# A kernel that plans its own instruction order: when a tile counts as free is taken from all its operations, not from the one scheduled last

## The chip, the cores and the metric

The kernel runs on one core of one Trainium2 chip. The metric is device time in microseconds (us) of one execution; lower is better. Three runs of the kernel before and one profiled execution of it are at hand.

## The reference

Attention with capped scores, followed by two dense stages, all in float32. `q`, `k`, `v` have shape 4 x 12 x 448 x 64 (48 heads).

```
s = cap * tanh(q @ k.T / 8 / cap);  p = exp(s - max);  a = p / sum(p) @ v
x = heads of a side by side                 # 1792 tokens x 768
h = x @ w_in;  x = (h * cos(h)) @ w_out     # 768 -> 2048 -> 768
x = ((x @ w1) * (x @ w2)) @ w3 @ w_out2     # 768 -> 1024 -> 1024 -> 768
```

The weights come as 64-bit floats and are turned into float32 on the chip.

## The kernel before

**Numbers.** Most products are made at more than one multiplication's precision: each operand is split into a high part (a cast to the reduced-width float32 that TensorE takes) and a low part (what the cast left), and three matmuls (high by high, high by low, low by high: `mm3`, lines 389 to 391) are summed. So each weight and each activation needs a copy and a subtraction before TensorE can use it. The scores of the first four pairs of heads are made from plain float32 operands instead (`SLIM = 4`, line 604); both kernels do this.

**Stages.** Scores, tanh and exp of a pair of heads (lines 640 to 665), products with `v` (684, 689), division by the row sums, split (`a_out`); beside it `make_w34` multiplies `w3` and `w_out2` into one matrix. From about 180 us `moe1` runs beside what is left of attention: per unit TensorE makes `h` (`bank<-xh,wih`), the chain of `cos` runs on ACT, DVE and POOL (`hs`, `w`, `kk`, `g`), and TensorE multiplies by `w_out` (`bank<-g,woh`). The last stage, `moe2`, begins near 730 us.

**A weight's way** (`f64`, line 925, and `convert`, line 896). SP loads the 64-bit words (`raw` or `rawc`); ACT or POOL scales the high word (903, 904); POOL or DVE begins the float32 value in tile `x` or `wx` (line 909); DVE adds bits twice (916, 920). Then three operations read that tile: a transfer to DRAM (`spill`, issued by SP on line 385, so that a later pass need not convert again: `wi_d`, `wo_d`), the copy to the high part (`copy`, lines 365, 366 and 369), and the subtraction for the low part (`lo`, line 375). There are two tiles `x` and two tiles `wx`. In `rights` (line 1200) the same is done with four tiles `stl` and the transfer `w_d`.

**The order of the work.** The program first makes a list of operations with due times, costs and the engines on which each may run. `Plan.schedule` then plays them through in time with these costs: at each step it takes the operations in order of due time, and starts those whose inputs are ready, whose engine is idle and for which each new tile has a free slot in its ring. The sequence it finds is the order of the instructions; on the chip each engine runs its own in that order, and waits where a tile isn't free yet. A transfer is costed as 0.66 us on SP, then `kb / 250` on a common line, then 2.2 us:

```
out = end
if o.kb:
    line = max(line, end) + o.kb / self.RATE
    out = line + self.LATENCY
```

and `HOP` is 0.25 us. A tile goes back to its ring when the last of its operations has been scheduled.

Of the kernel before, what the change touches and what calls it, by code (L numbers as in the profile page):

```python
# [45 lines left out]
class Ref:  # L46
    def __init__(self, item, sub=None, pick=None):
        self.item, self.sub, self.pick = item, sub, pick
# [12 lines left out]

class Item:
    def __init__(self, ring):
        self.ring, self.slot, self.ops, self.first = ring, None, 0, None
        self.writers, self.readers = {}, {}

    def tile(self):
# [70 lines left out]
class Plan:  # L138
# [57 lines left out]
    def schedule(self):  # L196
        for o, after, before in self.events:
            for p in after:
                o.deps.update(p.users)
            for p in before:  # L200
                for u in set(p.users):
                    u.deps.add(o)
        for n, o in enumerate(self.ops):
            o.left = len(o.deps)
            for d in o.deps:
                d.nexts.append(o)
        free = dict(PE=1.0, ACT=2.0, DVE=3.4, POOL=1.5, SP=1.2, port=0.0)

        def port(x):
            return x[0] == "POOL" or len(x) > 3  # L210

        free[None] = 0.0
        table, order, t, line = "exp", [], 0.0, 0.0
        cands = [(o.due, n, o) for n, o in enumerate(self.ops) if o.left == 0]
        num = {o: n for n, o in enumerate(self.ops)}
        soon = []
        cands.sort(key=lambda c: c[:2])
        done, end_all = 0, 0.0
        busy = {e: 0.0 for e in free}
        while done < len(self.ops):  # L220
            while soon and soon[0][0] <= t + 1e-9:
                _, n, o = heapq.heappop(soon)
                cands.append((o.due, n, o))
            cands.sort(key=lambda c: c[:2])
            idle = {e for e in free if free[e] <= t + 1e-9}
            wait, rest, again, short = {}, [], False, set()
            for c in cands:
                o = c[2]
                if o.table and table and o.table != table and o.due > t - SLACK_T and any(
                        x[2].table == table for x in cands):  # L230
                    rest.append(c)
                    continue
                pick = min(o.opts, key=lambda x: max(free[x[0]] - t, free["port"] - t if port(x) else 0.0, 0.0) + wait.get(x[0], 0.0) + x[1] * (PAR.get("w" + (x[0] or ""), 1.0) if o.due < PAR["tw"] else 1.0))
                if pick[0] in idle and port(pick) and free["port"] > t + 1e-9:
                    pick = None
                elif pick[0] not in idle:
                    if len(o.opts) == 1:
                        wait[pick[0]] = wait.get(pick[0], 0.0) + pick[1] * PAR["back"]
                    pick = None
                need = {}  # L240
                for it in o.allocs:
                    need[it.ring] = need.get(it.ring, 0) + 1
                lack = {r for r, n in need.items() if sum(x[0] <= t + 1e-9 for x in r.free) < n}
                if pick is None or any(it.slot is None and it.first is not o for it in o.uses if it.ring) or any(
                        not r.loose and r.queue[0].first is not o for r in need) or lack or short & need.keys():
                    short |= {r for r in lack if r.loose}
                    rest.append(c)
                    continue
                for it in o.allocs:
                    it.ring.queue.remove(it)  # L250
                    it.slot = heapq.heappop(it.ring.free)[1]
                (e, cost, f), two = pick[:3], port(pick)
                if o.table:
                    if table != o.table:
                        cost += self.SWITCH
                    table = o.table
                end = t + cost
                if e is not None:
                    free[e] = end
                    idle.discard(e)  # L260
                    busy[e] += cost
                    if two:
                        free["port"] = end
                        busy["port"] += cost
# [4 lines that stand above are left out]
                end_all = max(end_all, out)  # L269
                if o.move is not None:  # L270
                    for k in o.move[1](o.allocs[0].slot):
                        heapq.heappush(o.move[0].free, (out, k))
                for it in o.uses:
                    it.ops -= 1
                    if it.ops == 0 and it.ring is not None:
                        heapq.heappush(it.ring.free, (out + (self.HOP if e else 0.0), it.slot))
                for x in o.nexts:
                    x.left -= 1
                    x.ready = max(x.ready, out + (self.HOP if e else 0.0))
                    if x.left == 0:  # L280
                        heapq.heappush(soon, (x.ready, num[x], x))
                order.append((t, f))
                done += 1
                again = again or e is None
            cands = rest
            if again:
                continue
            times = [x for x in free.values() if x > t + 1e-9]
            if soon:
                times.append(soon[0][0])  # L290
            times += [r.free[0][0] for r in self.rings if r.free and r.free[0][0] > t + 1e-9]
            if done < len(self.ops):
                assert times, [(c[0], [(it.ring.tag, it.ring.queue[0] is it, it.ring.free) for it in c[2].allocs])
                               for c in cands[:20]]
                t = max(t, min(times))
        self.time, self.busy = end_all, busy
        return order
# [1098 lines left out]
```

## Time and profile before

| what | value |
|---|---|
| three runs, median (lowest, highest) | 1071.6 us (1068.7, 1073.46) |
| the profiled execution, time | 1074.96 us |
| its span in the profile | 1073.2 us |
| TensorE busy (PE) | 1052.1 us, 98% |
| VectorE busy (DVE) | 860.9 us, 80% |
| ScalarE busy (ACT) | 492.9 us, 46% |
| GpSimd busy (POOL) | 177.5 us, 17% |
| granted TensorE clock, mean | 0.994 |

Times in the trace count from the start of the span. PEld is TensorE's weight load, SPq the queue of SyncE, which issues the transfers. "a <- b" names the tile written and the tiles read, with buffer numbers left out. PEclk is the granted TensorE clock as a share of its full 2.4 GHz.

### The profile page before, as it was taken

What the parts mean: (1) busy time and instruction counts of PE and PEld (TensorE: products, weight loads), DVE (VectorE), ACT (ScalarE), POOL (GpSimd) and SP (SyncE); (2) the same over time, 40 slices, a digit from 0 to 9 for tenths busy, and PEclk for the clock granted to TensorE, in tenths of its full rate; (3) what the DMA queues carried; (4) which work ended last, traced back from release to release, by engine and by line L of the source; (5) the groups of instructions that cost most, each with busy time, mean ns of one, the idle gap of its engine ahead of it and who ended that gap; (6) DMA issues with size and microseconds to landing.
All of it is one profiled execution on the core that took longest, in us unless ns stands there. A gap on an engine that the chain in (4) does not pass through costs nothing.

```text
span 1073.2 us, 15589 instructions
## 1 busy us (share of the span) xinstructions
PE 1052.1 (98%) x5808; PEld 892.4 (83%) x5808; DVE 860.9 (80%) x1317; ACT 492.9 (46%) x653; POOL 177.5 (17%) x165
## 2 busy tenths in 40 slices
PE   7999999999999999999999999999999999999997
PEld 2676775777777888889999999999999999999996
DVE  5888667897998999778789987779899889767642
ACT  6687666776676775632253211112443245311121
POOL 4221211321341222210001100011313100000000
PEclk9999998999999999999999999999999999999999
DMA  8866965866766764527633411205555446221132
GB/s 253 215 211 177 247 179 162 224 179 206 220 201 205 230 172 148 174 61 250 211 119 104 148 49 55 60 15 175 198 193 195 155 124 220 102 89 59 60 108 86
DMA packets 82120, 167.38 MB, mean 156 GB/s; under 512 B 19571, under 2 KB 55411, under 8 KB 82035
## 3 DMA queue, kind: packets, MB, share of 16 engines
q1 hardware_dynamic: 82034, 166.30, 50.7%
q8 instruction: 47, 0.77, 0.3%
q14 instruction: 39, 0.31, 0.1%
HBM read 127.47 MB, written 38.62 MB: 155 GB/s over the span
## 4 chain that ended last, share of the span: by engine, by line
PE 83%; DVE 7%; DMA 4%; issue 2%; ACT 1%; POOL 1%; SPq 1%; DVEq 0%; POOLq 0%; ACTq 0%
PE bank L389 24%; PE bank L391 24%; PE bank L390 24%; PE bank L684 5%; PE double L650 2%; PE double L651 2%; PE bank L689 2%; DMA raw<-in_w3T 1%; DMA wo_d<-wx 1%; DMA raw<-in_w_out 1%; SPq L385 1%; DMA rb<-rs_d 1%; DVE wx L916 1%; DVE ks L375 1%; DVE ql L375 1%
## 5 line engine op out<-in xcount | busy, mean ns | idle before, releaser
L389 PE MATMUL bank<-g,woh 128*128 128x448 f32 x384 | 140.2, 365 | 2.0 <-ACT zs L365 2.0
L389 PE MATMUL bank<-xh,wih 128*128 128x448 f32 x384 | 140.1, 365 | 0.9 <-DVE y L366 0.9
L391 PE MATMUL bank<-xh,wil 128*128 128x448 f32 x384 | 139.6, 364 | 0.0
L391 PE MATMUL bank<-g,wol 128*128 128x448 f32 x384 | 139.4, 363 | 0.0
L390 PE MATMUL bank<-xl,wih 128*128 128x448 f32 x384 | 139.0, 362 | 0.0
L390 PE MATMUL bank<-g,woh 128*128 128x448 f32 x384 | 138.7, 361 | 0.0
L375 DVE TENSOR_TENSOR y<-bank,y 128x448 f32<-128x448 f32 x168 | 103.4, 617 | 42.4 <-PE bank L391 41.3
L365 ACT COPY hs<-bank 128x448 f32<-128x448 f32 x73 | 39.0, 536 | 180.7 <-PE bank L391 180.5
L665 ACT ACTIVATE double<-double,ts 112x896 f32<-112x896 f32 x96 | 93.7, 982 | 61.6 <-PE double L651 52.7
L665 ACT ACTIVATE p<-double,pac 112x896 f32<-112x896 f32 x96 | 96.2, 1013 | 1.6
L389 PEld LDWEIGHTS bank<-g,woh 128*128 128x128 f32 x384 | 72.0, 188 | 12.6 <-ACT zs L365 2.4
L684 PE MATMUL bank<-p,v 112*32 112x448 f32 x768 | 80.9, 562 | 0.0
L389 PEld LDWEIGHTS bank<-xh,wih 128*128 128x128 f32 x384 | 72.3, 188 | 8.7 <-issue 2.2
L391 PEld LDWEIGHTS bank<-xh,wil 128*128 128x128 f32 x384 | 72.4, 188 | 5.2
L390 PEld LDWEIGHTS bank<-xl,wih 128*128 128x128 f32 x384 | 72.2, 188 | 5.1
L391 PEld LDWEIGHTS bank<-g,wol 128*128 128x128 f32 x384 | 72.1, 188 | 5.2
L390 PEld LDWEIGHTS bank<-g,woh 128*128 128x128 f32 x384 | 71.9, 187 | 4.9
L389 PE MATMUL bank<-ab,w34h 128*128 128x448 f32 x192 | 69.7, 363 | 0.0
L391 PE MATMUL bank<-ab,w34l 128*128 128x448 f32 x192 | 69.5, 362 | 0.0
L390 PE MATMUL bank<-ab,w34h 128*128 128x448 f32 x192 | 69.3, 361 | 0.0
L684 PEld LDWEIGHTS bank<-p,v 112*32 112x32 f32 x768 | 22.9, 113 | 47.0 <-issue 45.1
L650 PE MATMUL double<-qh,ks 128*112 128x448 f32 x160 | 59.5, 372 | 2.4 <-ACT p L665 2.2
(230 smaller groups left out, 2351.1 us busy)
## 6 DMA issues: line engine op xcount, KB each, us to landing
rawc<-in_w_out SPq DMA_DIRECT2D x16, 768.0 KB, 5.8
stq<-w_d SPq DMA_DIRECT2D x32, 384.0 KB, 3.2
rawc<-in_w_in SPq DMA_DIRECT2D x13, 768.0 KB, 5.2
qr<-in_q SPq DMA_DIRECT2D x41, 224.0 KB, 4.6
kr<-in_k SPq DMA_DIRECT2D x41, 224.0 KB, 4.3
raw<-in_w3T SPq DMA_DIRECT2D x16, 512.0 KB, 5.7
rawl<-in_w SPq DMA_DIRECT2D x10, 768.0 KB, 4.8
raw<-in_w_out SPq DMA_DIRECT2D x8, 768.0 KB, 6.6
```

What stands on the lines that cost most here:

```text
L365: "A": ("ACT", (0.051 if psum else 0.094) + n / 1200, lambda: ACT.copy(dst(), src())),
L375: "D": ("DVE", 0.068 + n / 960, lambda: DVE.tensor_tensor(dst(), a(), b(), op=op))
L385: plan.op(due, [("SP", 0.66, lambda: SP.dma_start(dst(), src()))], r=r, w=w, kb=kb)
L389: PE.matmul(out, wh, xh, start=first, stop=False, skip_group_check=on)
L390: PE.matmul(out, wh, xl, start=False, stop=False, skip_group_check=on)
L391: PE.matmul(out, wl, xh, start=False, stop=last, skip_group_check=on)
L650: PE.matmul(o, w, qh(), start=True, stop=False)
L651: PE.matmul(o, w, ql(), start=False, stop=True)
L665: lambda f=f, x=x, o=o: ACT.activation(o(), s(), f, scale=x[:CP]))],
L684: PE.matmul(pv()[q * Q:(q + 1) * Q, :S], w()[:, j, c, d:d + Q], piece(j, c), **flags)
L689: PE.matmul(z()[q:q + Q, :S], one(), piece(j, 2 * c + k), start=c == 0, stop=c == NT - 1)
L916: DVE.scalar_tensor_tensor(xi, h_(), 3, xi, op0=ALU.logical_shift_left, op1=ALU.bitwise_or)
```

## The change

Each tile keeps the latest end of the operations scheduled on it so far (`it.free`), and that time, not the end of the operation scheduled last, is when its slot goes back to the ring. The two differ where an operation scheduled earlier ends later. Nothing is added to or taken from the list of operations, their costs, due times or rings.

```
 class Item:
     def __init__(self, ring):
-        self.ring, self.slot, self.ops, self.first = ring, None, 0, None
+        self.ring, self.slot, self.ops, self.first, self.free = ring, None, 0, None, 0.0
...
                 for it in o.uses:
                     it.ops -= 1
+                    it.free = max(it.free, out + (self.HOP if e else 0.0))
                     if it.ops == 0 and it.ring is not None:
-                        heapq.heappush(it.ring.free, (out + (self.HOP if e else 0.0), it.slot))
+                        heapq.heappush(it.ring.free, (it.free, it.slot))
```

## Rows read from the trace of the kernel before

**Rows 1.** The page: the span and the engines' busy times.
```profile
span 1073.2 us, 15589 instructions
PE 1052.1 (98%) x5808; PEld 892.4 (83%) x5808; DVE 860.9 (80%) x1317; ACT 492.9 (46%) x653; POOL 177.5 (17%) x165
```

**Rows 2.** Busy time of PE: stretch, length, busy (instructions), clock, DMA share, GB/s.
```profile
0.00:54.00 54.00, 45.48 (x279) 1.00 0.83 233
...
150.00:300.00 150.00, 144.35 (x889) 0.97 0.68 197
300.00:1053.00 753.00, 753.00 (x3930) 1.00 0.43 138
```

**Rows 3.** What PE waited for, 150 to 300 us: total us, times, longest.
```profile
PE double L650 <- ACT p L665: 2.2, 1, 2.2
PE bank L389 <- ACT zs L365: 2.0, 1, 2.0
PE bank L389 <- DVE y L366: 0.9, 1, 0.9
PE bank L391 <- DVE w3l L375: 0.5, 1, 0.5
```

**Rows 4.** The chain that ended last, 140 to 190 us: start, us, what.
```profile
153.79 5.82 DMA wi_d<-x
...
167.33 0.71 PE double L650
...
169.17 5.38 PE bank L684 x32
...
178.02 0.20 PE double L651
...
185.05 3.14 PE bank L684 x32
```

**Rows 5.** Timeline of DVE, 150 to 165 us: idle before in brackets.
```profile
154.34 0.96 DVE L375 TENSOR_TENSOR wil<-x,wih 128x768 fp32r<-128x768 f32 x1
...
160.67 1.35 DVE L916 SCALAR_TENSOR_TENSOR x<-raw,x 128x768 uint32<-128x768 uint32 x1 [4.83 <-POOL x L909]
```

**Rows 6.** Timeline of ACT, 146 to 176 us.
```profile
164.53 0.83 ACT L365 CAST wih<-x 128x768 fp32r<-128x768 f32 x1 [4.40 <-DVE x L920]
```

**Rows 7.** The chain that ended last, 236 to 284 us.
```profile
239.55 8.89 DMA wo_d<-wx
...
273.42 0.54 DVE x L375
...
276.11 0.32 PE bank L390
...
279.41 0.29 PE double L651
```

**Rows 8.** Timeline of DVE, 226 to 282 us.
```profile
240.00 0.96 DVE L375 TENSOR_TENSOR wol<-wx,woh 128x768 fp32r<-128x768 f32 x1 [0.37 <-ACT woh L365]
...
249.53 1.62 DVE L916 SCALAR_TENSOR_TENSOR wx<-rawc,wx 128x768 uint32<-128x768 uint32 x1 [5.09 <-POOL wx L909]
```

**Rows 9.** Timeline of SP's queue, 226 to 282 us.
```profile
232.54 1.32 SPq L385 DMA_DIRECT2D kr<-in_k  x2
...
239.17 0.34 SPq L385 DMA_DIRECT2D rawc<-in_w_in  x1
```

**Rows 10.** Transfers: issues, KB each, median us from issue to landing.
```profile
wo_d<-wx SPq DMA_DIRECT2D x16, 384.0 KB, 2.9
...
w_d<-stl SPq DMA_DIRECT2D x16, 384.0 KB, 2.6
...
wi_d<-wx SPq DMA_DIRECT2D x13, 384.0 KB, 5.0
```

**Rows 11.** What POOL waited for, whole span: total us, times, longest.
```profile
POOL xh L369 <- PE bank L390: 103.5, 5, 43.0
...
POOL wih L369 <- PE bank L391: 34.2, 1, 34.2
...
POOL x L909 <- DMA wi_d<-x: 11.8, 1, 11.8
...
POOL wx L909 <- DMA wo_d<-wx: 6.4, 2, 5.6
```

**Rows 12.** Busy time of all engines by stretch: PE, PEld, DVE, ACT, POOL.
```profile
270.00:297.00 27.00, 25.01 (x136) 20.63 (x132) 26.41 (x36) 18.18 (x23) 9.57 (x9) 0.94 0.73 224
```

More of the change, by code (lines that the diff above doesn't have):

```diff
@@ L63, in __init__ @@
     def __init__(self, ring):
-        self.ring, self.slot, self.ops, self.first = ring, None, 0, None
+        self.ring, self.slot, self.ops, self.first, self.free = ring, None, 0, None, 0.0
         self.writers, self.readers = {}, {}
@@ L274, in schedule @@
                     it.ops -= 1
+                    it.free = max(it.free, out + (self.HOP if e else 0.0))
                     if it.ops == 0 and it.ring is not None:
-                        heapq.heappush(it.ring.free, (out + (self.HOP if e else 0.0), it.slot))
+                        heapq.heappush(it.ring.free, (it.free, it.slot))
                 for x in o.nexts:
```

## The prediction

> **What bounds the kernel now.** I read the page first: TensorE is busy in 1052.1 of 1073.2 us, DVE in 860.9 [rows 1], so only 21.1 us are to be had unless TensorE's own work gets shorter. Then the busy time by stretch, to place the idle time: 8.52 us lie in the first 54 us, 5.65 between 150 and 300, none in the 753 us from 300 to 1053 [rows 2], and what is left is mostly the end. Then PE's waits between 150 and 300: four, of 2.2, 2.0, 0.9 and 0.5 us [rows 3]. Last the chain that ended last, to see what these four hang on: each goes back to one of two transfers to DRAM, `wi_d<-x` at 153.79 [rows 4] and `wo_d<-wx` at 239.55 [rows 7].
>
> **First place.** `wi_d<-x` was issued at 153.79 and landed 5.82 us later, at 159.61 [rows 4]. The last reader of that tile on an engine, the subtraction `wil`, had ended at 155.30 [rows 5]. The next user of the slot, POOL's line 909, stood waiting for the transfer [rows 11]; DVE stood idle for 4.83 us behind POOL [rows 5], ACT for 4.40 us behind DVE, at the cast `wih` [rows 6]. Both engines run in order, so the tanh and exp behind the cast came late, and TensorE, short of score tiles, waited 2.2 us; the subtraction `w3l`, queued on DVE behind line 916, gave the 0.5 us [rows 3]. After the wait the matmuls ran at the lower of TensorE's two clock levels (1.2 GHz instead of 2.4): four score matmuls fill the chain from 167.33 to 169.17, 1.84 us where four take 0.81 at 0.20 each, and the 32 of line 684 took 5.38 us where they take 3.14 at the full clock [rows 4]. That is 1.03 + 2.24 = 3.3 us. The place costs 2.2 + 0.5 + 3.3 = 6.0 us.
>
> **Second place.** `wo_d<-wx`, 239.55 to 248.44 [rows 7]; `wol`, the last engine reader, ended at 240.96, and DVE stood idle 5.09 us until POOL had the slot [rows 8]. From then on DVE is never free again before the step `x` at 273.42 (the chain there is DVE's almost without a break) [rows 7], and what it hands over comes late: a `y` copy (0.9 us of PE) and, over ACT, `zs` (2.0 us) [rows 3]. Ten matmuls after it, from 276.11 to 279.70, ran at the lower clock (the first and the last of the ten stand in [rows 7]): 3.59 us against 2.03, so 1.6. The place costs 0.9 + 2.0 + 1.6 = 4.5 us. Together 10.5 us.
>
> **What the change does, part by part.** It adds no instruction and takes none away; only order and slot numbers can move. A slot's time changes only where an operation scheduled earlier ends later than the last. That is not so for a chain (each step needs the one before), nor for tiles whose last operation is itself the transfer (`y`, `sum`, `ob`, `zs`, `rs`): nothing there. Where two engines read the same tile the difference is under a microsecond of planned time, and I cost it at nothing, under TensorE's backlog; without that cover it would be under 1 us at each place. `xsh` and `xsl` also feed transfers, but by the kernel's due times (`p1`, four steps of 3.03 us a pair) their next writer comes 12 us later or more: nothing. What stays is the tile that is spilled while it is split: `x`, `wx` and `stl`, of which 16, 13 and 16 spills stand in the view [rows 10], with three more of `wi_d<-x`.
>
> How far the slot moves in the plan, from the kernel's constants: let the value be ready at T. Copy and subtraction on DVE end at T + 0.25 + 0.47 + 0.25 + 0.87, so the old slot time is T + 2.09. The transfer ends at T + 0.25 + 0.66 + 1.57 + 2.2, so the new one is T + 4.93: 2.8 us later with an empty line, and more by what is queued. About the second place SP had issued, from 232.54 to 239.17, four loads of 230, two of 115 and two of 768, and a spill of 393 (the first and the last of these nine stand in [rows 9]); with the spill itself that is 13.9 us at 250 per us, so the planned landing is 232.54 + 0.66 + 13.9 + 2.2 = 249.3, where the trace has 248.44 [rows 7]. So the plan foresees the long landing as well as the short one.
>
> The moved step is POOL's line 909, DVE's 916 and 920, a cast, a subtraction, the spill itself on SP, and the next load of 64-bit words, which waits for `raw` to come free. In the plan what was queued behind it is put ahead of it. At the first place tanh and exp (0.89 us each by the kernel's costs, one pair after the other) go ahead of the cast; to clear PE's 2.2 us half of ACT's 4.40 is enough. At the second, 5.09 us of other work go ahead, against 2.9 us of PE waits. The conversion itself starts no sooner and no later than the landing allows. So I count both places as cleared. Bounds for this: below, a gain of 0 (the same wait met by another instruction); above 10.5, all waits of PE in that stretch with their clock; more cannot be gained there. I take 10, near the upper end, since at both places the released time exceeds the wait.
>
> To the same effect for the loads: SP's queue is moved past too, since a later conversion holds `raw` and `rawc` longer and the next load, issued in order, could be late by the 2.8 us. It is hidden as long as weights are ahead of TensorE. They are: POOL stood waiting for TensorE to release `wih` (34.2 us) and `xh` (103.5 us), and not the reverse [rows 11]. If that cover is gone, a late weight costs what a place costs here, 4.5 to 6.0 us.
>
> One rule speaks against the change. The spills land after a median of 2.9, 2.6 and 5.0 us [rows 10], the planner counts at least 0.66 + 1.57 + 2.2 = 4.43, so most tiles are now held in the plan 1.5 us longer than on the chip. The Trainium skill, "DMA: Bandwidth & Descriptors", section "Anatomy of one DMA", puts a transfer (issued from GpSimd) at about 2.0 us plus bytes at 436 GB/s, which is an estimate of 2.9 us for this size. By that rule the first spill would have landed near 156.7, 1.4 us behind `wil`, there would be little to gain and the kernel would stay at about 1071.6; by the rows it took 5.82, and 10.5 us are to be had. The medians agree with the page, the two places that matter don't.
>
> **The sum.** 1074.96 - 10 = 1065.0 in terms of the profiled execution, which is 3.4 us above the median of the runs. If the runs have the same two stalls, the median becomes 1061.6; if they are shorter because theirs are milder, it stays near 1065. I take 1064, nearer the upper, since some remainder of a wait is likely.
>
> **Rivals.**
> *One place stays, or a like one opens.* The cast `wih` can end up ahead of the exp again, or another of the spills in the loaded stretch can stall DVE, which is at 26.41 of 27 us there [rows 12]. For it: a greedy order shifts everything behind its first difference. Against: the plan now has the long landing. With the first place kept the gain is 4.5: 1067 to 1070.5; with the second kept, 6.0: 1065.5 to 1069.
> *The change does nothing that counts.* POOL's line 909 meets the same landing in the same place among its neighbours; 1070 to 1073. Against: a shift of 2.8 us is longer than any operation behind it. The page's rule would leave the time here, too.
> *Slower: conversions too late.* The 1.5 us by which the usual spill is now overstated, 48 times, lets weights and the split tiles of `moe2` slip behind TensorE between 300 and 1053, where it has no idle time now [rows 2], so that any stall there is new. Its price is that of a place here, 4.5 to 6.0 us, clock included. With 10 us gained it takes more than two such stalls to lose; three give 1066 to 1070 with the full gain, and 1076 to 1080 if the places of now are only shifted, five 1075 and up. For it: DVE's load. Against: the waits for TensorE in [rows 11]. It decides once a weight's lead falls below some 2 us.
>
> **How the numbers follow.** Forecast 0.55, one place or a like one 0.20, nothing 0.10, late conversions 0.15. Within 0.5% of 1071.6, about what a measurement of this kernel can tell from no change (the three runs differ by 0.44%), is 1066.2 to 1077. Faster than that: the forecast but for 0.03, and 0.06 of the one place: 0.58. Slower: 0.12 of the late conversions. The rest, 0.30, is the same. The range goes from 1059.5, all 10.5 us off the median and 1.6 more for the difference between runs, to 1075, which leaves out most of the slower rival; the forecast's own is 1061 to 1066.
>
> **What would show it.** Up to about 150 us nothing moves: the same start, with 8.5 us idle in the first 54. The waits of POOL for `wi_d<-x` and `wo_d<-wx` (11.8 and 6.4 us) shrink below 2 us, PE's idle time between 150 and 300 falls from 5.65 to below 1.5 and the clock there to 1.00. After the `p` at about 159 ACT runs a tanh before the cast `wih`. From 300 to 1053 PE stays without idle time. The prediction is wrong if a PE wait with a lower clock stands in another place, on `wih`, `woh`, `xh` or a bank that DVE empties late, or if these two transfers still hold POOL for more than 4 us.

## The result and the profile after

The changed kernel takes 1060.95 us (median of five runs, 1059.46 to 1062.77), the kernel before 1071.24 (1068.7 to 1073.46): a ratio of 0.9908, 95% interval 0.9887 to 0.9928. That is 10.3 us of the medians; 1064 was forecast, within 1059.5 to 1075.

The page of the changed kernel, as in [rows 1], and then TensorE's busy time by stretch, as in [rows 2]:

```profile
span 1060.2 us, 15586 instructions
...
PE 1045.2 (99%) x5808; PEld 890.4 (84%) x5808; DVE 861.1 (81%) x1330; ACT 491.1 (46%) x649; POOL 164.5 (16%) x156
```

```profile
0.00:54.00 54.00, 45.57 (x285) 1.00 0.84 242
...
150.00:300.00 150.00, 150.00 (x947) 1.00 0.74 214
300.00:1053.00 753.00, 753.00 (x3929) 1.00 0.43 135
```

The 5.65 us of idle time between 150 and 300 us are gone, the lower clock with them, and nothing came in their place: from 300 to 1053 TensorE still has no idle time. Everything that TensorE now waits for in the whole span, but a small rest, stands in the first 54 us or in the last few (columns as in [rows 3]):

```profile
PE double L641 <- DMA qr<-in_k: 5.6, 1, 5.6
PE double L641 <- ACT p L666: 2.9, 2, 2.0
PE bank L392 <- DVE w3l L376: 0.2, 1, 0.2
```

All line numbers from 275 on are one higher than before. POOL no longer waits for `wi_d` or `wo_d` at all; the two waits of [rows 11] have no line in the changed kernel's view. The first place there, on the timelines of POOL, DVE and ACT:

```profile
155.70 0.62 POOL L370 TENSOR_SCALAR w3h<-x 128x512 fp32r<-128x512 f32 x1 [8.65 <-PE bank L391]
157.67 1.73 POOL L910 TENSOR_SCALAR x<-raw 128x768 f32<-128x768 f32 x2 [1.36 <-DVE w3l L376]
```

```profile
156.90 0.68 DVE L376 TENSOR_TENSOR w3l<-x,w3h 128x512 fp32r<-128x512 f32 x1
158.58 1.63 DVE L917 SCALAR_TENSOR_TENSOR x<-raw,x 128x768 uint32<-128x768 uint32 x1 [0.99 <-POOL x L910]
```

```profile
163.18 1.01 ACT L666 ACTIVATE p<-double,pac 112x896 f32<-112x896 f32 x1
164.30 0.98 ACT L666 ACTIVATE double<-double,ts 112x896 f32<-112x896 f32 x1
165.21 0.82 ACT L366 CAST wih<-x 128x768 fp32r<-128x768 f32 x1
```

DVE's idle time before its first bit step is 0.99 us where it was 4.83 [rows 5], and ACT runs tanh and exp without a break up to the cast, before which it had stood 4.40 us [rows 6]. POOL is released by `w3l`, not by a transfer: the planner gave the conversion the other of the two tiles `x`, whose last reader ended at 157.6, and put the copy `w3h`, which had stood behind the waiting conversion, ahead of it.

The chain of the changed kernel shows where the time was saved:

```profile
164.26 3.14 PE bank L685 x32
...
177.92 3.14 PE bank L685 x32
```

The first of these corresponds to the line at 169.17 us with 5.38 us, the second to the one at 185.05 [rows 4]: the changed kernel is 4.9 us ahead when the value products of the first place begin, and 7.1 us ahead when the next ones begin. Of the 13.0 us between the two spans 0.9 came before either place and is not the change's. It arose at TensorE's first value products, here before and after:

```profile
14.25 2.87 PE L684 MATMUL bank<-p,v 112*32 112x448 f32 x16 
```

```profile
14.17 1.98 PE L685 MATMUL bank<-p,v 112*32 112x448 f32 x16 
```

The order of work is still the same there; in the profiled execution of the kernel before these products were slower, presumably by the lower clock level (no row gives the granted clock there). The medians, which differ by 10.3 us, are what the change is to be judged by.

### The profile page after: what moved, and what is told of

It reads as the page before. It is cut to its first block, busy times and chain, and to the rows that moved or that the text cites. A ratio compares the mean times of both kernels' runs of the same rounds, so it can differ in the third digit from the quotient of the medians.

```text
span 1060.2 us, 15586 instructions
## 1 busy us (share of the span) xinstructions
PE 1045.2 (99%) x5808; PEld 890.4 (84%) x5808; DVE 861.1 (81%) x1330; ACT 491.1 (46%) x649; POOL 164.5 (16%) x156
## 4 chain that ended last, share of the span: by engine, by line
PE 96%; DMA 2%; ACT 1%; DVE 1%; SPq 0%; issue 0%; DVEq 0%; ACTq 0%
PE bank L390 27%; PE bank L392 26%; PE bank L391 26%; PE bank L685 7%; PE bank L690 3%; PE double L651 3%; PE double L652 3%; PE double L641 1%; DMA rb<-rs_d 1%; DMA raw<-in_w3T 1%; ACT p L666 0%; DMA qr<-in_k 0%; ACT double L666 0%; SPq L386 0%; DVE w3l L376 0%
## 5 line engine op out<-in xcount | busy, mean ns | idle before, releaser
L685 PE MATMUL bank<-p,v 112*32 112x448 f32 x768 | 77.8, 544 | 0.0
```

The costliest lines, as they stand in the source:

```text
L685: PE.matmul(pv()[q * Q:(q + 1) * Q, :S], w()[:, j, c, d:d + Q], piece(j, c), **flags)
```

## The experiments

Each was timed beside the kernel before on the same chip; ratios are to that kernel, with 95% intervals. In the planner, the rule applied to all tiles but `x` and `wx` gives every engine the sequence that it had (only slot numbers of `stl` move): what the change does, it does through these two rings.

**The old order without the two late spills.** Not issued are the transfers that held POOL at the two places; the planner still counts them, so every other instruction stands where it stood.

```
+ drop = (kind, fc) in (("i", 0), ("o", 2))      # in moe1.weight; second pass reads w34_d
...
- dma(due - 4, spill, x, ...)
+ plan.op(due - 4, [("SP", 0.66, lambda: None)], r=[x], w=[spill], kb=393)
```

> The kernel before, its order untouched, but two of its 48 spills are not issued (the first of w_in, which held POOL at 153.8 us, and the one of w_out issued at 239.6); the second pass then loads those two weights from another array, so this kernel leaves out two writes and computes with two wrong weights. Wait theory: the two landings were what the kernel lost its time to, so with the old order the time falls by the 10.5 us of the two places, to about 1061, and PE's idle time between 150 and 300 us falls from 5.65 to under 1. Rival, the new order as a whole is what is faster (engines, copies and loads fall differently): with the old order kept the time stays within 1069 to 1073.

Measured: 1062.06 us, ratio 0.9905 (0.9880 to 0.9930). TensorE's busy time by stretch:

```profile
150.00:200.00 50.00, 50.00 (x352) 1.00 0.70 192
200.00:250.00 50.00, 49.86 (x296) 1.00 0.70 209
250.00:300.00 50.00, 50.00 (x297) 1.00 0.73 213
```

With the order of before and without two of its transfers the kernel is as fast as the changed one, within what the runs resolve. So the loss was the wait for these two landings; the rival "the new order as a whole" falls for this pair of kernels. The edit also takes away 0.8 MB of traffic, which is hardly the reason: the changed kernel moves all of it and is as fast.

**One spill at a time.** The same edit with `("i", 0)` alone, and with `("o", 2)` alone.

> The kernel before with its order, without the first spill of w_in alone (its second pass loads that weight from another array). The rule for x alone had given all 10.6 us, the rule for wx alone 4.4 us. Theory A: the two places add up, and the rule for x cleared the second only because it also changed the order there; then with the old order the second place stays: 6 us less, about 1065.7, with PE waits of some 2.9 us near 257 and 273. Theory B: the second place is partly a consequence of the first (work that the first held up on DVE and ACT); then about 1061 to 1063 with those waits gone.

> The kernel before with its order, without the spill of w_out issued at 239.6 us alone. Theory A (they add up): 4.5 us less, about 1067.3; PE's waits of the first place stay (2.2 and 0.5 us with the lower clock after it). Theory B gives the same here; a time of 1070 or more would say that the second landing was not what held up DVE.

Without the first: 1066.04 us, ratio 0.9953 (0.9936 to 0.9970). Without the second: 1067.15, ratio 0.9966 (0.9949 to 0.9982). The first kernel's waits of PE and of POOL, then the second's:

```profile
PE bank L389 <- ACT zs L365: 2.5, 2, 1.9
...
POOL wx L909 <- DMA wo_d<-wx: 11.2, 3, 6.4
```

```profile
PE double L650 <- ACT p L665: 2.6, 2, 2.2
...
POOL x L909 <- DMA wi_d<-x: 11.7, 1, 11.7
```

In each the place whose spill was kept is still there, with the wait of [rows 3] that belonged to it. By the ratios the first is worth 5.0 us (3.2 to 6.9), the second 3.6 (1.9 to 5.5); together 8.6, against 10.2 (7.5 to 12.9) with both out. Theory A holds: the two add up, within the intervals.

**The rule for one ring at a time.**

```
- heapq.heappush(it.ring.free, (it.free, it.slot))
+ last = out + (self.HOP if e else 0.0)
+ heapq.heappush(it.ring.free, (it.free if it.ring.tag == "x" else last, it.slot))   # or "wx"
```

> The new rule for the tiles x alone (the first place). Wait theory: the first place goes and the second stays, unless the changed order behind the first moves it: 6.0 us less, about 1065. Rival, the gain belongs to the order as a whole: no fixed share; anything from 1060 to 1072, with no link to the two waits.

> The new rule for the tiles wx alone (the second place). Wait theory: the first place stays with its wait of POOL for wi_d<-x and the lower clock, the second goes: 4.5 us less, about 1066.7. Rival, the order as a whole: no fixed share.

For `wx` alone: 1067.42, ratio 0.9958 (0.9943 to 0.9974), 4.5 us as expected, with POOL's wait for `wi_d<-x` (11.7 us) still there. For `x` alone: 1061.17, ratio 0.9900 (0.9875 to 0.9925), which is the whole gain and not the 6 us expected. Its waits of POOL for spills:

```profile
POOL wx L911 <- DMA wo_d<-wx: 3.2, 1, 3.2
POOL wx L911 <- DMA wi_d<-wx: 2.4, 1, 2.4
```

Tiles `wx` still go back too early in this plan, and POOL still waits for their transfers, but TensorE waits for none of it. Whether that is because these waits are shorter or because nothing urgent stands behind them was not tested. So a slot time that is wrong need not cost anything; it costs where the wait reaches TensorE through the engines queued behind it.

**Half of the shift.** The slot counts as free midway between old and new time: `last + 0.5 * (it.free - last)`.

> The slot is counted free halfway between the old time and the new one. Wait theory: the plan's landing of the second place lies some 7 us behind the old slot time and 3 us at the first; half of it leaves waits of some 1.5 to 4 us, which the lead of ACT and DVE may cover or not: between 1061 and 1068, with POOL waits for wi_d or wo_d of about half of the old ones. If any other order would do, 1061 and no such waits.

1066.46 us, ratio 0.9951 (0.9932 to 0.9969). Its waits:

```profile
PE double L652 <- ACT p L667: 3.4, 2, 2.7
...
POOL wx L911 <- DMA wo_d<-wx: 7.6, 2, 6.6
POOL wx L911 <- DMA wi_d<-wx: 7.5, 2, 7.3
POOL x L911 <- DMA wi_d<-x: 2.3, 1, 2.3
```

At the first place POOL's wait is down from 11.8 to 2.3 us and PE's is gone. But the 2.7 us that PE waits later do not go back to a spill. They end at 211.23 us; POOL's two long waits for spills end behind that, at 216.49 and 246.44, and TensorE has no wait after them. The chain in front of PE's wait is DVE's and ACT's own work, and no transfer stands in it back to 140 us:

```profile
207.26 2.43 DVE x L377
209.71 0.57 ACT xh L367
210.27 0.92 ACT p L667
211.23 0.71 PE double L652
```

DVE's `x` took 2.4 us here, where it took 0.62 at 154.28 in the changed kernel; POOL ran `ql` beside it (from 206.65, 2.54 us), but what made it long was not tested. So the time fell into the expected range for another reason than the expected one: the waits for spills were not halved, and they cost nothing. Not any other order will do, as the wait theory said; but an order can also lose some 5 us without a late spill.

**Still later.** Spilled tiles count as free 6 and 9 us later than in the changed kernel.

```
+ late = 6.0 if it.free > last and it.ring.tag in ("x", "wx") else 0.0     # or 9.0
+ heapq.heappush(it.ring.free, (it.free + late, it.slot))
```

> The changed kernel, with spilled tiles x and wx counted free 6 us later still. The question is how much lateness the weights bear, the rival on the slow side in the prediction. If weights run ahead of TensorE by more than 6 us, the time stays at 1061 within 2 us; if the lead is about 2 us, as that rival had it, new waits of PE with a lower clock stand on wih, woh or on the copies behind them, at 4.5 to 6 us each: 1070 or more.

> Spilled tiles x and wx counted free 9 us later than in the changed kernel. At 6 us later the time was 2.5 us longer, with three PE waits of 0.5 to 0.7 us. If the weights' lead is being used up, the waits grow by about 3 us in all or more, with a lower clock: 1066 to 1075. If those small waits were an accident of that order: 1060 to 1064.

6 us: 1063.45, ratio 0.9924 (0.9899 to 0.9950). 9 us: 1060.89, ratio 0.9912 (0.9884 to 0.9940). PE's waits that the changed kernel does not have, at 6 us and then at 9:

```profile
PE bank L393 <- DVE xl L378: 0.7, 1, 0.7
PE bank L392 <- DVE zs L369: 0.5, 1, 0.5
PE double L653 <- ACT p L668: 0.5, 1, 0.5
```

```profile
PE double L653 <- ACT p L668: 0.3, 1, 0.3
```

The 6 us kernel is 2.5 us above the changed one, a little more than the 2 us expected, which the intervals do not resolve. Nothing grows with the lateness: 9 us late is as fast as in time, so the waits at 6 us belong to that order. The weights do come later: at 9 us the last spill of `w_in` is issued at 460.8 us, in the changed kernel at 435.6, and still TensorE has no idle time from 150 to 300 us and less than 1 us from 300 to 1053. So the weights' lead over TensorE is far more than 2 us. The rival on the slow side has no ground in this kernel.

**Two other orders, each with the old and the new rule.** `HOP` 0.20 in place of 0.25; then `t0` 10.4 in place of 10.0. Both give another order well before the first place.

> The kernel before with the planner's HOP at 0.20 us in place of 0.25, which gives another order from the first 20 us on. With its partner, the changed kernel at 0.20, it asks if the gain is more than the luck of one order. Wait theory: POOL again waits for a spill's landing in this one, and the partner is faster by what those waits cost PE here, be it 2 or 10 us. Rival: the pair's difference has no link to such waits and may as well be of the other sign. Against the kernel before: anywhere from 1060 to 1085.

> The changed kernel with HOP at 0.20 us. Wait theory: not slower than its partner, faster by the partner's losses to spills that land late, and with less than 1 us of PE waits between 150 and 300 us that go back to a spill. Rival: as likely slower as faster than the partner.

> A second pair in another order: the kernel before with all due times of attention 0.4 us later (t0 10.4 in place of 10.0). At HOP 0.20 the old rule had no wait of POOL for a spill and lost nothing to one, and the new rule made 1 us. If the gain is the losses to spills in the order at hand: the more POOL waits here for wi_d or wo_d with DVE idle behind it, the more the partner gains, and nothing where there are none. Rival: the new rule's order is faster by some 10 us or slower whatever such waits there are.

> The changed kernel with t0 at 10.4. Wait theory: 1060 to 1064, without PE waits that go back to a spill, and the difference to its partner is what the partner lost to spills. Rival: the difference has another place than these waits.

| | old rule | ratio | new rule | ratio |
|---|---|---|---|---|
| `HOP` 0.20 | 1063.63 | 0.9930 (0.9902 to 0.9957) | 1062.64 | 0.9922 (0.9896 to 0.9948) |
| `t0` 10.4 | 1063.52 | 0.9925 (0.9901 to 0.9950) | 1063.15 | 0.9924 (0.9900 to 0.9948) |

The partners differ by 1.0 and 0.4 us, which their intervals do not resolve. At `HOP` 0.20 the old rule, against the expectation, has no wait of POOL for a spill: there is nothing to gain. At `t0` 10.4 the old rule has the first place, with the full clock behind it, and the new rule removes it but has POOL wait for another spill; the waits of PE and POOL with the old rule, then with the new:

```profile
PE double L650 <- ACT p L665: 2.2, 1, 2.2
...
POOL x L909 <- DMA wi_d<-x: 11.7, 1, 11.7
```

```profile
PE bank L390 <- ACT zs L366: 1.5, 2, 1.0
...
POOL wx L910 <- DMA wi_d<-wx: 11.1, 1, 11.1
```

The last two lines do not belong together: PE's waits end at 217.34 and 290.36 us, POOL's at 265.44, and DVE has no idle time while POOL waits. So the rule does not make POOL's waits impossible (the plan's landing is an estimate, and the chip's came later), but this one cost nothing. Of the 2.2 us that the new rule took from PE's waits at the first place, 1.5 came back in waits with another cause.

Most of the 10 us could thus be had with the old rule as well: in an order that misses both collisions, and in one that keeps the first but loses only the 2.2 us of the wait to it. The four kernels are in keeping with the wait theory, but they do not confirm it: their differences are too small.

## Why the prediction was right

**What bounded the kernel** was right, and the chain read to the right two transfers: taking these two out, and nothing else, gives the changed kernel's time within what the runs resolve.

**The sum** came out in total, 10 us counted and 10.3 measured, but partly by luck. It was made for the profiled execution, and there the gain is larger. Of the 13.0 us between the two spans 0.9 arose at the start, 6.2 (7.1 less 0.9) at the first place, where 6.0 was counted, and 5.9 behind it, where 4.5 was counted for the second; some 1.4 us have no term in the prediction, and "more cannot be gained there" was too strict. On the other hand it counts 3.3 + 1.6 us for the lower clock, as that execution had it, and most runs had less. Of 37 timed runs of the kernel before, the nine with a granted clock of 0.995 or less took 1070.8 to 1074.3 us (median 1073.9), the eight at 0.999 took 1067.7 to 1070.1 (median 1069.4). The latter lose some 8.5 us against the changed kernel, where the counted waits alone come to 5.6. So the sum has too much clock and too little of something else, and the two nearly cancel; what the rest is stays open. By leaving out one spill at a time the first place is worth 5.0 (3.2 to 6.9) and the second 3.6 (1.9 to 5.5), by the rule for `wx` alone the second is worth 4.5. The pull from 1061.6 up to 1064 for "some remainder of a wait" was wrong: no remainder was left.

**The parts costed at nothing** (tiles whose last operation is the transfer, chains, tiles read by two engines, `xsh`) were right, and `stl` too: without `x` and `wx` the order is the same. That the loads are covered was right, even with slots that count as free 9 us later.

**One step was wrong.** "The conversion itself starts no sooner and no later than the landing allows": at the first place it starts at 157.67 us and not at 159.75, 2.1 us sooner, of which 0.9 came from the start, because the planner took the other tile, which `w3l` frees. Knowing the true slot time changed the choice of the tile, not only the place in the queue. What that is worth by itself no run separates; ACT's and DVE's standing still, on which the forecast rested, went as predicted. Nor was it order and slot numbers alone that moved: the planner also gave operations to other engines (POOL has 156 instructions where it had 165, DVE 1330 where it had 1317).

**The rule that spoke against the change** foresaw spills that land in some 2.9 us, and little to gain. Of the three medians that the prediction says agree with that, the third, 5.0 us [rows 10], does not. In the changed kernel they are 2.6 to 5.4 us, columns as in [rows 10]:

```profile
wo_d<-wx SPq DMA_DIRECT2D x16, 384.0 KB, 4.4
...
w_d<-stl SPq DMA_DIRECT2D x16, 384.0 KB, 2.6
...
wi_d<-wx SPq DMA_DIRECT2D x13, 384.0 KB, 5.4
```

The two landings that decided took 5.82 and 8.89 us [rows 4, 7], and taking them out was worth 10 us.

**The slower rival** had its size wrong: a lead of "some 2 us" was feared, and 9 us of extra lateness cost nothing. Its sums were wrong as well: three stalls at 4.5 to 6.0 us are 13.5 to 18 us, which gives 1075 and up with the full gain; 1066 to 1070 is the price of one. The forecast did not rest on this.

## What to carry to other kernels

A list scheduler that hands a slot back at the end of the last-scheduled reader must also know the slower reader scheduled before it, above all a transfer out of the tile: on the chip an in-order engine will stand at the next writer, and everything queued behind it stands too. Look for it as a wait of a lightly loaded engine on a transfer out, followed by the idle time of a full one, and price it by the wait that ends at the bounding engine; some 11.7 us of POOL's waiting cost 2 to 6 us at the first place, and 11.1 us elsewhere cost nothing. Before crediting such a rule with the whole gain, try it in a second order: here two small changes of a constant gave 7.5 and 8.0 of the 10 us with the old rule. And follow each new wait of the bounding engine back by the chain before it is put down to the cause that was looked for: at half the shift it had another.

## What the runs showed of the hardware that was not expected

The same wait of TensorE was followed by the lower clock level (1.2 GHz) in some executions and not in others. At the first place PE waits 2.2 us for the same exp in four profiled kernels that keep the place. The 32 value products behind it took 5.38 us in the kernel before [rows 4] and 4.84 without the second spill, but the full-clock 3.14 us with the rule for `wx` alone and in the old rule at `t0` 10.4; the chains of these three:

```profile
167.04 4.84 PE bank L684 x32
```

```profile
166.48 3.14 PE bank L686 x32
```

```profile
167.08 3.14 PE bank L684 x32
```

What a wait costs beyond itself is therefore not fixed: 0 to 3.3 us at this place. The timed runs of the kernel before point the same way: by their granted clocks, 0.993 to 0.999, they differ by some 4.5 us (figures under "The sum" above). The start looks alike, as far as durations without a granted clock can tell: the first value products took 2.87 us in one profile and 1.98 in the other with the same order. The Trainium skill, "TensorE: Matmul & The Clock Gate", section "Part 1: The HAM clock gate", says of a kernel's start that the number of matmuls at the lower rate differs from run to run; the two starts agree with it, and the waits in mid-kernel behave likewise.
